# First loads, decay tables and head sums of a retention and two-layer MoE kernel

## The chip, the cores and the metric

One core of one Trainium2 chip runs the whole kernel. The metric is device time in microseconds (us), the median of several executions of the same program. Engines are named as the profile names them: PE is the matmul engine (PEld its weight loads), DVE the vector engine, ACT the scalar engine, POOL the general one, SP the engine that issues most transfers.

## The reference

Retention (attention with a decay in place of softmax) over 4 batches, 8 heads, 576 tokens and head width 64, then two dense layers over 2304 tokens of width 512. All is fp32.

```python
scores = scale * np.matmul(q, k.transpose(0, 1, 3, 2))
Dmat = np.where(rel >= 0, gamma[:, None, None] ** rel[None, :, :], 0.0)   # rel = i - j
attn = np.matmul(scores * Dmat[None], v)                 # then (tokens, 512)
h = attn @ w_in;  x = (h * np.cos(h)) @ w_out            # 512 -> 2048 -> 512
xn = x / np.sqrt(np.mean(x * x, -1) + 1e-6) * rms_g
g = xn @ w_gate                                          # 512 -> 1536
out = (g * (1.0 / (1.0 + np.exp(-g))) * (xn @ w_val)) @ w_out2
```

## The kernel before

**Retention.** Each batch is cut into five chunks of tokens, four of 128 and one of 64, so there are 20 chunks. The decay is split into factors: v is scaled once per chunk on POOL (L244) by a table in `gk_sb`, and the result is scaled on DVE (L283) by a table `gam[c]`. `gam[0]` is the loaded `gam0`; `gam[1]` to `gam[4]` are made from it on ACT, four activations each (L237), issued where the chunk is loaded. `scores(n)` makes the masked scores of a chunk: eight fp32 matmuls of contraction 64, two heads side by side on two halves of the array's rows (L249), and two DVE multiplications by the mask (L252). `values(n)` adds the chunk's sum of keys and values to `total` in PSUM (L265, four matmuls of 128x128, each covering two heads, of which only the two 64x64 blocks on the diagonal are ever read), multiplies the state of earlier chunks by q (L270), copies `total` into `state` on ACT (L275, two copies of 64x256), and adds the chunk's own part (L280, eight matmuls, one per head, with 64 weight columns each, two heads on two halves of the array's columns). An fp32 matmul appears in the profile as two matmul records.

**Order of the start.** `load(0)` brings chunk 0 in four pieces of 256 KB (keys, queries, values, keys by token), with the small tables between them, all seven on SP's queue (L226). Chunks 1 and on are one transfer of 1 MB (L228); the short chunks are two (L230, L231). Ten matmuls on a tile of ones (L290, `WARM`) run before the first data arrive. The first five chunks run in a prologue, then two chunks stand beside each of the first eight steps of the first layer.

**First layer.** A step is one tile of 512 tokens with one block of 128 of the 2048 hidden columns: products of operands split in a high and a low fp32r part, three matmuls for each (`mm3`, L187 to L189), cosine and product on DVE and ACT (L414 to L424). During the first 16 steps the weights, stored as 64-bit numbers, are turned into fp32 and split: `Block.convert`, with L132, L141 and L159 on ACT and L136, L137, L142, L143 and L124 on DVE. `split_x` (L181 and L124) splits the tokens. A scheduler lays out the order of each engine's instructions at build time by priorities and its own estimates, and each engine then works in that order; the later stages of ACT, DVE and POOL, from the end of step 15, are in an order written out by hand.

Of the kernel before, what the change touches and what calls it, by code (L numbers as in the profile page):

```python
# [22 lines left out]
F32 = mybir.dt.float32  # L23
# [3 lines left out]
AF = mybir.ActivationFunctionType  # L27
# [3 lines left out]
P = 128  # L31
B, H, S, D = 4, 8, 576, 64
# [5 lines left out]
NPAIR = H // 2  # L38
NFULL = S // P
REST = S - NFULL * P  # L40
NCH = NFULL + 1
# [18 lines left out]
NSLOT_B = NW1 - NSLOT_A  # L60
ATT_STEPS = 8
CONV_LEAD = 3
WARM = 10
AHEAD = 4
LAG = 3
LAST_BEGINS = [48, 51, 54, 65, 66, 67]
# [9 lines left out]
def body(ctx: ExitStack, tc, qkv, qkr, vr, w1, w2, rg, gq, gk, mask, out):  # L76
    nc = tc.nc
# [19 lines left out]
    psa = att.enter_context(tc.tile_pool(name="psa", bufs=1, space=PSUM, reuse_waits="tile"))  # L97
# [11 lines left out]
    def ps_tile():  # L109
        if "psh" not in late:  # L110
            return psa.tile([P, 512], F32, tag="g", bufs=3, name="g")
        taken[0] += 1
        return hidden_tile() if taken[0] % 2 else acc_tile(KC + taken[0] // 2 % 2)

    mask_sb = const.tile([P, P], F32, name="mask_sb")
# [51 lines left out]
    def temps():  # L167
        return cvp.tile([P, 2, 512], I32, tag="w", name="t")
# [32 lines left out]
    ap1 = att.enter_context(tc.tile_pool(name="ap1", bufs=1, reuse_waits="tile"))  # L201
# [3 lines left out]
    width = lambda c: P if c < NFULL else REST  # L205
    ld, sc, total = {}, {}, {}
    gam0 = ap1.tile([P, NPAIR, P], F32, name="gam0")
    gam = [gam0]
    PRO = NCH
    gk_sb = ap1.tile([P, NCH * (H + NPAIR)], F32, name="gk_sb")  # L210
    vg_sb = gk_sb[:, :NCH * H].rearrange("p (c h) -> p c h", c=NCH)
    later = gk_sb[:, NCH * H:].rearrange("p (c a) -> p c a", c=NCH)
    state = ap1.tile([P, NPAIR, P], F32, name="state")
# [5 lines left out]
    def load(n):  # L219

        b, c = chunks[n]
        x = wa.tile([P, 4, DM], F32, tag="w", name="x")
        if n == 0:
            for src, dst in ((qkv[b, c, :, 0], x[:, 0]), (qkv[b, c, :, 1], x[:, 1]), (gk, gk_sb), (mask, mask_sb),
                             (qkv[b, c, :, 2], x[:, 2]), (gq, gam0), (qkv[b, c, :, 3], x[:, 3])):
                nc.sync.dma_start(dst, src)  # L226
        elif c < NFULL:
            nc.sync.dma_start(x, qkv[b, c])  # L228
        else:
            nc.sync.dma_start(x[:, :2, :NPAIR * REST], qkr[b])  # L230
            nc.sync.dma_start(x[:REST, 2], vr[b])  # L231
        blocks = lambda a: a[:, :NPAIR * width(c)].rearrange("p (a i) -> p a i", a=NPAIR)
        ld[n] = blocks(x[:, 0]), blocks(x[:, 1]), x[:, 2], x[:, 3]
        if 0 < n < NCH:
            gam.append(ap1.tile([P, NPAIR, width(c)], F32, name=f"gam{c}"))
            for p in range(NPAIR):
                nc.scalar.activation(gam[c][:, p, :], gam0[:, p, :width(c)], AF.Copy, scale=later[:, c, p:p + 1])  # L237

    def scores(n):
        b, c = chunks[n]  # L240
# [15 lines left out]
    def values(n):  # L256
        b, c = chunks[n]
        w = width(c)
        _, qt, vv, kk = ld.pop(n)
        if c < NFULL:  # L260
            if c == 0:
                total[0] = psa.tile([P, NPAIR, P], F32, tag="st", name="total")
            for p in range(NPAIR):
                cs = slice(p * P, (p + 1) * P)
                nc.tensor.matmul(total[0][:, p, :], kk[:, cs], vv[:, cs], start=c == 0 and p == 0, stop=True,  # L265
                                 skip_group_check=True)
        po = ps_tile().rearrange("p (a i) -> p a i", a=NPAIR)
        if c > 0:
            for p in range(NPAIR):
                nc.tensor.matmul(po[:, p, :w], state[:, p, :], qt[:, p, :], start=p == 0, stop=False,  # L270
                                 skip_group_check=True)
        if c < NFULL:
            for hh in range(2):
                r = slice(hh * D, (hh + 1) * D)
                nc.scalar.copy(state[r, :, r], total[0][r, :, r])  # L275
        for p in range(NPAIR):
            for hh in range(2):
                h = 2 * p + hh
                r = slice(hh * D, (hh + 1) * D)
                nc.tensor.matmul(po[r, p, :w], vv[:w, h * D:(h + 1) * D], sc[n, hh][:w, p, :w],  # L280
                                 start=c == 0 and p == 0, stop=True, skip_group_check=True)
        t0 = b * S + c * P
        nc.vector.tensor_tensor(xall[:, :, t0:t0 + w], po[:, :, :w], gam[c], op=ALU.mult)  # L283
        del sc[n, 0], sc[n, 1]
# [3 lines left out]
    idle_bank = psp.tile([P, 512], F32, tag="acc0", name="idle_bank")  # L288
    for _ in range(WARM):
        nc.tensor.matmul(idle_bank, ones_r, warm, start=True, stop=True)  # L290
    plan = list(PLAN)

    def fetch(until):

        while plan and until not in ld:
            n = plan.pop(0)
            if n < 0:
                blocks1.append(Block(w1[len(blocks1)], wa))
            else:
                load(n)  # L300
# [3 lines left out]
    for n in range(PRO):  # L304
        fetch(n + AHEAD)
        scores(n + 1)
        values(n)
        if n == 3:
            split_x(ORDER_A[0])
            blocks1[0].convert(temps())  # L310
# [316 lines left out]
    for i in range(LAST + LAG):  # L627
# [12 lines left out]
        if i < LAST:  # L640
            t, f = steps[i]
# [278 lines left out]
```

## Time and profile before

| | us |
|---|---|
| median of 3 runs | 930.67 |
| lowest and highest run | 929.98, 932.38 |
| the profiled execution, its own time | 928.54 |
| span of that execution, first to last instruction | 926.7 |
| PE busy in the span | 903.1 |
| DVE busy in the span | 619.6 |
| ACT busy in the span | 462.2 |

The profiled execution is 2.13 us below the median and outside the range of the three runs; 1.84 us of its time lie outside the span. All stretches below are in us from the start of the span. PE is busy nearly everywhere, DVE mainly in the first 165 us, so shares over the whole span say little about the stretch in which the change lies, which is the first 130 us.

### The profile page before, as it was taken

To read this page: it belongs to the slowest core of one execution; us is meant where nothing else is said; L and a number is where in the kernel's file an instruction comes from. 1 tells how busy PE (TensorE), PEld (TensorE's weight loads), DVE (VectorE), ACT (ScalarE), POOL (GpSimd) and SP (SyncE) were. 2 spreads that over 40 slices of the span, in tenths; PEclk is the share of its full clock that TensorE was granted. 3 is DMA by queue.
4 is the path that set the end of the run, shared out by engine and by line. 5 is a ranking of instruction groups with operands and counts; after the bars stand their busy time and mean duration, and the time that the engine had idled before them with its cause. 6 is when DMAs were issued, how large, how long until landed. Compare 5 with 4: busy or idle time off the path is not lost.

```text
span 926.7 us, 12891 instructions
## 1 busy us (share of the span) xinstructions
PE 903.1 (97%) x4996; PEld 791.0 (85%) x4996; DVE 619.6 (67%) x1022; ACT 462.2 (50%) x816; POOL 26.9 (3%) x27
## 2 busy tenths in 40 slices
PE   7999999999999999999999899999999999999998
PEld 6777788888887888988888799999888999999997
DVE  3999989778888887768657666675456446333332
ACT  4656566576556666367545444444432334322222
POOL 2321100000000000000000000000000000000000
PEclk9999999999999999999999999999999999999999
DMA  8946451035424353202035376676744555755531
GB/s 334 410 186 227 155 224 72 21 117 193 164 98 159 137 159 126 69 1 103 1 148 204 124 297 251 252 268 246 259 176 176 207 209 212 265 206 209 204 132 69
DMA packets 34732, 163.72 MB, mean 177 GB/s; under 512 B 4080, under 2 KB 5232, under 8 KB 23792
## 3 DMA queue, kind: packets, MB, share of 16 engines
q1 hardware_dynamic: 34672, 162.91, 48.0%
q8 instruction: 39, 0.64, 0.3%
q14 instruction: 21, 0.17, 0.1%
HBM read 123.57 MB, written 39.32 MB: 176 GB/s over the span
## 4 chain that ended last, share of the span: by engine, by line
PE 79%; DVE 14%; ACT 4%; issue 2%; DMA 1%; SPq 0%; ACTq 0%; DVEq 0%
PE h L743 27%; PE acc L715 15%; PE acc L187 8%; PE acc L188 8%; PE acc L189 8%; PE h L189 3%; PE h L188 3%; PE h L187 3%; DVE r L421 1%; DVE t L142 1%; DVE t L143 1%; PE g L280 1%; DVE r L415 1%; PE g L249 1%; PE g L270 1%
## 5 line engine op out<-in xcount | busy, mean ns | idle before, releaser
L743 PE MATMUL h<-w 128*128 128x384 f32 x1224 | 230.5, 337 | 6.6 <-ACT s L750 2.6
L743 PEld LDWEIGHTS h<-w 128*128 128x128 f32 x1224 | 214.9, 188 | 15.2 <-ACT s L750 5.3
L715 PE MATMUL acc<-w,shi 128*128 128x512 f32 x432 | 134.3, 392 | 0.0
L187 PE MATMUL acc<-ghi,w 128*128 128x512 f32 (+1 forms) x320 | 117.4, 373 | 2.8 <-ACT xall L614 1.7
L188 PE MATMUL acc<-glo,w 128*128 128x512 f32 (+1 forms) x320 | 117.6, 369 | 0.1
L189 PE MATMUL acc<-ghi,w 128*128 128x512 f32 (+1 forms) x320 | 117.3, 368 | 0.0
L750 ACT COPY s<-h 128x384 f32<-128x384 f32 x108 | 51.9, 480 | 128.1 <-PE h L743 128.0
L715 PEld LDWEIGHTS acc<-w,shi 128*128 128x128 f32 x432 | 80.1, 188 | 13.4
L417 ACT ACTIVATE r<-r,half_pi 128x512 f32<-128x512 f32 (+1 forms) x80 | 54.5, 681 | 65.5 <-DVE r L415 65.2
L763 DVE TENSOR_TENSOR sg<-s,h 128x384 f32<-128x384 f32 x54 | 29.9, 553 | 85.6 <-PE h L743 45.4
L715 PE MATMUL acc<-w,slo 128*128 128x512 f32 x216 | 85.4, 395 | 0.0
L775 ACT CAST shi<-v 128x384 fp32r<-128x384 f32 x72 | 37.0, 514 | 70.3 <-DVE v L771 70.3
L124 DVE TENSOR_TENSOR glo<-r,ghi 128x512 fp32r<-128x512 f32 (+1 forms) x78 | 49.6, 636 | 33.4 <-ACT ghi L423 31.6
L187 PEld LDWEIGHTS acc<-ghi,w 128*128 128x128 f32 x320 | 59.4, 188 | 14.5 <-ACT xall L614 2.8
L423 ACT CAST ghi<-r 128x512 fp32r<-128x512 f32 (+1 forms) x80 | 46.2, 577 | 48.2 <-DVE r L421 46.9
L189 PEld LDWEIGHTS acc<-ghi,w 128*128 128x128 f32 x320 | 60.3, 188 | 10.1
L188 PEld LDWEIGHTS acc<-glo,w 128*128 128x128 f32 x320 | 60.3, 188 | 10.1 <-DVE glo L124 0.3
L124 DVE TENSOR_TENSOR slo<-v,shi 128x384 fp32r<-128x384 f32 x72 | 40.1, 557 | 37.3 <-ACT shi L775 37.3
L770 DVE TENSOR_TENSOR v<-s,h 128x384 f32<-128x384 f32 x54 | 29.8, 552 | 52.0 <-PE h L743 37.9
L743 PE MATMUL h<-b,w 128*128 128x384 f32 x288 | 56.8, 338 | 0.0
L188 PE MATMUL h<-xlo,w 128*128 128x512 f32 (+1 forms) x148 | 54.3, 367 | 0.1
L189 PE MATMUL h<-xhi,w 128*128 128x512 f32 (+1 forms) x148 | 54.2, 366 | 0.0
(105 smaller groups left out, 1518.6 us busy)
## 6 DMA issues: line engine op xcount, KB each, us to landing
w<-s SPq DMA_DIRECT2D x24, 1024.0 KB, 4.8
raw<-w_dram SPq DMA_DIRECT2D x36, 512.0 KB, 4.0
w<-w SPq DMA_DIRECT2D x18, 1024.0 KB, 5.1
w<-s SPq DMA_DIRECT2D x24, 768.0 KB, 6.4
raw<-w_dram SPq DMA_DIRECT2D x16, 1024.0 KB, 7.1
x<-qkv_dram SPq DMA_DIRECT2D x15, 1024.0 KB, 8.1
s<-w SPq DMA_DIRECT2D x12, 1024.0 KB, 4.8
s<-w SPq DMA_DIRECT2D x12, 768.0 KB, 3.6
```

The source lines that it names most:

```text
L124: eng.tensor_tensor(dst, src, hi.bitcast(F32), op=ALU.subtract)
L187: nc.tensor.matmul(dst, a[0], b[0], start=start, stop=False)
L188: nc.tensor.matmul(dst, a[0], b[1], start=False, stop=False)
L189: nc.tensor.matmul(dst, a[1], b[0], start=False, stop=stop)
L417: nc.scalar.activation(r, r, AF.Sin, bias=half_pi, scale=1.0)
L423: nc.scalar.copy(hi, r)
L715: nc.tensor.matmul(acc, (hi, hi, lo)[k][:, c], w[:, u, (0, 1, 0)[k], :], start=start and u == 0 and k == 0, stop=stop and u == 1 and k == 2)
L743: nc.tensor.matmul(bank, a[:, wp], xp[:, c], start=start and kc == 0 and n == 0, stop=kc == 1 and n == 2, skip_group_check=True)
L750: nc.scalar.copy(t, alpha)
L763: nc.vector.tensor_tensor(t, s, bank, op=ALU.add)
L770: nc.vector.tensor_tensor(t, s, bank, op=ALU.add)
L775: nc.scalar.copy(hi, t)
```

## The change

The first chunk comes in two transfers of 512 KB on SP's queue, and the three tables go out on ACT's queue, beside them. Chunk 1 comes in two halves, each with a semaphore of its own. The warm-up has eight matmuls in place of ten. The decay tables are written out after `values(n)` in place of at the load. The head sums are eight matmuls of 64x64 in place of four of 128x128: `total` is half as wide, each head writes its own half of the partitions, and ACT reads a contiguous block. Work on DVE and POOL keeps its count and its sizes.

```diff
-WARM = 10
+WARM = 8
...
         if n == 0:
-            for src, dst in ((qkv[b, c, :, 0], x[:, 0]), (qkv[b, c, :, 1], x[:, 1]), (gk, gk_sb), (mask, mask_sb),
-                             (qkv[b, c, :, 2], x[:, 2]), (gq, gam0), (qkv[b, c, :, 3], x[:, 3])):
-                nc.sync.dma_start(dst, src)
+            for eng, src, dst in ((nc.sync, qkv[b, c, :, :2], x[:, :2]), (nc.scalar, gk, gk_sb),
+                                  (nc.scalar, mask, mask_sb), (nc.sync, qkv[b, c, :, 2:], x[:, 2:]),
+                                  (nc.scalar, gq, gam0)):
+                eng.dma_start(dst, src)
+        elif n == 1:
+            nc.sync.dma_start(x[:, :2], qkv[b, c, :, :2])
+            nc.sync.dma_start(x[:, 2:], qkv[b, c, :, 2:])
...
-        if 0 < n < NCH:
-            gam.append(ap1.tile([P, NPAIR, width(c)], F32, name=f"gam{c}"))
-            for p in range(NPAIR):
-                nc.scalar.activation(gam[c][:, p, :], gam0[:, p, :width(c)], AF.Copy, scale=later[:, c, p:p + 1])
+
+    def decay(c):
+
+        gam.append(ap1.tile([P, NPAIR, width(c)], F32, name=f"gam{c}"))
+        for p in range(NPAIR):
+            nc.scalar.activation(gam[c][:, p, :], gam0[:, p, :width(c)], AF.Copy, scale=later[:, c, p:p + 1])
+
+    half = lambda hh: slice(hh * D, (hh + 1) * D)
...
-                total[0] = psa.tile([P, NPAIR, P], F32, tag="st", name="total")
+                total[0] = psa.tile([P, NPAIR, D], F32, tag="st", name="total")
             for p in range(NPAIR):
-                cs = slice(p * P, (p + 1) * P)
-                nc.tensor.matmul(total[0][:, p, :], kk[:, cs], vv[:, cs], start=c == 0 and p == 0, stop=True,
-                                 skip_group_check=True)
+                for hh in range(2):
+                    h = 2 * p + hh
+                    cs = slice(h * D, (h + 1) * D)
+                    nc.tensor.matmul(total[0][half(hh), p, :], kk[:, cs], vv[:, cs], start=c == 0 and p == 0,
+                                     stop=True, skip_group_check=True)
...
         values(n)
+        if n + 1 < NCH:
+            decay(n + 1)
```

The scheduler's order moves with it. First SP and ACT at the start of the program; `x` is a chunk of q, k and v, `raw` a block of weights, `gam_91` the loaded table. Before, SP's first rows are:

```order
L226 DMA x<-qkv_dram 128x512 x2
L226 DMA gk_sb<-gk_dram 128x60
L226 DMA mask_sb<-mask_dram 128x128
L226 DMA x<-qkv_dram 128x512
L226 DMA gam_91<-gq_dram 128x512
L226 DMA x<-qkv_dram 128x512
L228 DMA x<-qkv_dram 128x2048 x3
L151 DMA raw<-w_dram 128x2048
```

Now SP's are:

```order
L227 DMA x<-qkv_dram 128x1024 x2
L229 DMA x<-qkv_dram 128x1024
L230 DMA x<-qkv_dram 128x1024
L232 DMA x<-qkv_dram 128x2048 x2
L151 DMA raw<-w_dram 128x2048
```

Chunk 1 stands third and fourth on SP's queue, where it stood eighth. ACT's first rows before, with the decay tables at L237 and the copies of `total` at L275:

```order
L237 ACT_TABLE_LOAD
L237 ACTIVATE gam_121<-gam_91,gk_sb 128x128 x4
L237 ACTIVATE gam_143<-gam_91,gk_sb 128x128 x4
L237 ACTIVATE gam_150<-gam_91,gk_sb 128x128 x4
L237 ACTIVATE gam_160<-gam_91,gk_sb 128x64 x4
L275 COPY state<-total 64x4x64 x4
L132 ACTIVATE t<-raw 128x1024
```

ACT's first rows now, where the tables are L243 and the copies L284:

```order
L227 DMA gk_sb<-gk_dram 128x60
L227 DMA mask_sb<-mask_dram 128x128
L227 DMA gam_91<-gq_dram 128x512
L243 ACT_TABLE_LOAD
L243 ACTIVATE gam_178<-gam_91,gk_sb 128x128 x4
L243 ACTIVATE gam_224<-gam_91,gk_sb 128x128 x4
L243 ACTIVATE gam_272<-gam_91,gk_sb 128x128 x4
L243 ACTIVATE gam_318<-gam_91,gk_sb 128x64 x3
L284 COPY state<-total 64x4x64 x2
L243 ACTIVATE gam_318<-gam_91,gk_sb 128x64
L284 COPY state<-total 64x4x64 x2
```

Three transfers are issued ahead of the table load, and one of the sixteen activations has moved behind the first copies; fifteen still stand ahead of them. PE in the first two chunks, before:

```order
L290 MATMUL idle_bank<-warm,ones_r 128x512 x10
L249 MATMUL g<-x 128x128 x8
L265 MATMUL total<-x 128x128 x4
L249 MATMUL g<-x 128x128 x8
L280 MATMUL g<-s_137,x 64x128
...
L265 MATMUL total<-x 128x128 x2
```

PE there now, where the lines are L298, L257, L275 and L288:

```order
L298 MATMUL idle_bank<-warm,ones_r 128x512 x8
L257 MATMUL g<-x 128x128 x16
L275 MATMUL total<-x 64x64 x8
L288 MATMUL g<-s_129,x 64x128
...
L275 MATMUL total<-x 64x64 x8
L257 MATMUL g<-x 128x128 x8
```

The scores of chunk 1 have moved ahead of the head sums of chunk 0. From there to the last chunk the rows of PE, DVE and ACT keep their kinds and counts, but many stand a few places earlier or later; behind the first 16 steps of the first layer the three engines' orders are the same as before.

## Rows read from the trace of the kernel before

**Rows 1.** Busy time in four stretches: length, each engine's busy us, clock, DMA.

```profile
0.00:20.00 20.00, 14.24 (x130) 11.63 (x130) 6.14 (x12) 8.05 (x22) 4.57 (x9) 1.00 0.88 323
20.00:120.00 100.00, 95.66 (x862) 79.26 (x859) 96.67 (x124) 59.74 (x84) 19.33 (x16) 0.98 0.63 239
120.00:165.00 45.00, 44.64 (x231) 37.03 (x230) 41.10 (x54) 29.65 (x38) 0.00 (x0) 1.00 0.39 153
165.00:926.70 761.70, 748.54 (x3782) 663.10 (x3780) 475.71 (x834) 364.72 (x673) 2.99 (x2) 1.00 0.46 166
```

**Rows 2.** Chain of work that ended last: start, length, what ran.

```profile
3.07 4.95 DMA gam<-gq_dram
...
35.24 0.43 PE g L189
...
119.51 0.57 issue
120.08 0.69 DVE xall L283
```

**Rows 3.** Timeline of the first 22 us: start, length, instruction, idle before.

```profile
2.10 4.59 PE L290 MATMUL idle_bank<-warm,ones_r 128*128 128x512 f32 x10 [2.10 <-DVE warm L287]
...
4.02 1.54 SPq L228 DMA_DIRECT2D x<-qkv_dram  x3
...
8.10 1.28 ACT L237 ACT_TABLE_LOAD   x1 [8.10 <-DMA gam<-gq_dram]
...
9.39 4.57 ACT L237 ACTIVATE gam<-gam,gk_sb 128x128 f32<-128x128 f32 x16
...
11.48 1.16 PE L249 MATMUL g<-x 64*128 64x128 f32 x16 [1.32 <-DMA x<-qkv_dram]
...
14.75 0.68 PE L265 MATMUL total<-x 128*128 128x128 f32 x4 [1.09 <-ACT state L275]
...
19.16 1.15 ACT L132 ACTIVATE t<-raw 128x1024 f32<-128x1024 f32 x1 [0.25 <-DMA raw<-w_dram]
...
21.41 0.90 DVE L136 TENSOR_SCALAR t<-t 128x1024 f32<-128x1024 f32 x1
```

**Rows 4.** Single microseconds of the start; last two columns DMA share and GB/s.

```profile
2.00:3.00 1.00, 0.90 (x2) 0.83 (x3) 0.00 (x0) 0.00 (x0) 0.00 (x0) 1.00 0.75 260
3.00:4.00 1.00, 1.00 (x4) 0.71 (x3) 0.00 (x0) 0.00 (x0) 0.00 (x0) 1.00 0.90 279
4.00:5.00 1.00, 1.00 (x4) 0.81 (x3) 0.00 (x0) 0.00 (x0) 0.00 (x0) 1.00 0.79 215
5.00:6.00 1.00, 1.00 (x3) 0.79 (x3) 0.00 (x0) 0.00 (x0) 0.00 (x0) 1.00 0.87 203
6.00:7.00 1.00, 1.00 (x8) 0.38 (x8) 0.00 (x0) 0.00 (x0) 0.00 (x0) 1.00 0.86 236
...
9.00:10.00 1.00, 0.97 (x8) 0.97 (x8) 0.10 (x1) 0.99 (x4) 0.00 (x0) 1.00 1.03 434
```

**Rows 5.** Timeline of PE: groups of one shape in a dense stretch.

```profile
20.11 1.16 PE L265 MATMUL total<-x 128*128 128x128 f32 x8
...
21.10 1.06 PE L270 MATMUL g<-x,state 128*128 128x128 f32 x8
...
22.09 1.09 PE L280 MATMUL g<-s,x 128*64 128x128 f32 x16
...
23.11 0.68 PE L249 MATMUL g<-x 64*64 64x64 f32 x16
...
23.73 1.16 PE L265 MATMUL total<-x 128*128 128x128 f32 x8
```

**Rows 6.** Longest waits of PE between 20 and 120 us: total, times, longest.

```profile
PE g L249 <- DVE r L421: 1.3, 1, 1.3
PE g L280 <- DVE s L252: 1.2, 1, 1.2
```

**Rows 7.** PE around a slow stretch: length, PE busy, granted clock, DMA.

```profile
35.00:36.00 1.00, 1.00 (x4) 0.50 1.05 444
```

More of the change, by code (lines that the diff above doesn't have):

```diff
@@ L273, in values @@
             for hh in range(2):
-                r = slice(hh * D, (hh + 1) * D)
-                nc.scalar.copy(state[r, :, r], total[0][r, :, r])
+                nc.scalar.copy(state[half(hh), :, half(hh)], total[0][half(hh)])
         for p in range(NPAIR):
@@ L278, in values @@
                 h = 2 * p + hh
-                r = slice(hh * D, (hh + 1) * D)
-                nc.tensor.matmul(po[r, p, :w], vv[:w, h * D:(h + 1) * D], sc[n, hh][:w, p, :w],
+                nc.tensor.matmul(po[half(hh), p, :w], vv[:w, h * D:(h + 1) * D], sc[n, hh][:w, p, :w],
                                  start=c == 0 and p == 0, stop=True, skip_group_check=True)
```

## The prediction

> **What bounds the kernel now.** I read the busy times by stretch first, then the chain of work that ended last, then the timeline of the start, then the waits. After 120 us PE is the bound: busy 44.64 of 45 us and then 748.54 of 761.7 [rows 1], and no instruction behind the first 16 steps changes its place. So the change can only decide how early that stretch begins, and a gain there is carried to the end. The hand-over is in the chain: at 120.08 us a DVE multiplication (L283) runs that PE waits for, and from there the chain is PE's [rows 2]. Between 20 and 120 us neither engine is alone the bound: DVE is busy 96.67 of 100 us and PE 95.66 [rows 1]. DVE has 3.33 us of idle time there, PE 4.34. They wait for each other in turn; PE's two longest waits there are both for DVE, 1.3 and 1.2 us [rows 6]. Before 20 us the bound is the arrival of data and of the decay tables. PE waits 1.32 us for chunk 1 at 11.48 us; the sums of chunk 1 wait until 14.75 us for ACT to copy the sums of chunk 0, and ACT is late because it began the tables only at 8.10 us, when `gam0` had landed, and worked on them until 13.96 (9.39 + 4.57) [rows 3]; the transfer of `gam0`, 4.95 us, heads the chain [rows 2]. The first conversion starts on ACT at 19.16 us, 0.25 us late for its block of weights, and on DVE at 21.41 us [rows 3].
>
> **Start, the transfers.** The bytes are the same, so what can be gained is the time in which the transfer engines were empty or slow. From 2 to 7 us the five rows move 260 + 279 + 215 + 203 + 236 GB/s times 1 us, that is 1.19 MB, at shares of 0.75 + 0.90 + 0.79 + 0.87 + 0.86, so 4.17 us of 5 are filled; from 9 us on the rate is 434 GB/s [rows 4]. Two bounds follow. If the new pieces only fill the empty part, everything behind them comes 0.83 us earlier. If pieces of 4 KB a row run at the rate of the 8 KB rows, 434 x 5 us is 2.17 MB, 0.98 MB more, which is worth 0.98 / 0.434 = 2.3 us. No row of before shows a piece of 4 KB a row; I take 1.8, nearer the upper end, because SP's queue no longer holds chunk 1 back. Before, it was issued at 4.02 us [rows 3] behind seven others; now it stands behind two, each about 0.46 us (4.02 less a start at 0.8, over seven), so at some 1.7 us.
>
> The Trainium skill bears on this. Its page "DMA: Bandwidth & Descriptors", section "Issuing engines are not separate DMA queues", says that transfers of all issuing engines run on the same 16 engines and that several issuers only save issue time. By that rule alone the term would be the empty 0.83 us and not 1.8, and the sum 1.0 us smaller. The trace speaks neither for nor against it, since before all transfers here were SP's; that rates differ with the row length is another matter, which the rule leaves open.
>
> **Start, the tables.** `gam0` is now ACT's third transfer in place of SP's sixth. Its issue moves from 3.07 us [rows 2] to about 1.7 us (two issues of 0.46 us ahead of it), so with the same 4.95 us to landing ACT starts 1.4 us earlier; if it lands in some 3 us, 3.3 earlier. Fifteen activations in place of sixteen stand ahead of the first copy, 4.57 / 16 = 0.29 us each [rows 3]. So the copy comes 1.7 to 3.6 us earlier, and the sums of chunk 1, which waited 1.09 us for it, with it. That writing `decay` behind `values` does not move the tables behind the copies costs nothing as long as the transfers are the later of the two. Both paths have to move for the conversions to start earlier, so the smaller one counts: **1.8 us**, between 0.8 and 2.3.
>
> **The warm-up.** Ten matmuls take 4.59 us [rows 3], so two less are 0.9 us. The first scores may start so much earlier, but the next thing PE can do is wait for chunk 1, now ahead of the sums of chunk 0. I count it at nothing; the wait for chunk 1 covers it. Were that cover gone, it would add up to 0.9 us to the gain.
>
> **Head sums.** Four matmuls of 128x128 take 0.99 us from their start to that of the next group (20.11 to 21.10) [rows 5]. The new eight have 64 weight columns and 64 streamed columns, and no row shows this shape with 128 rows of contraction. Two rows bound it. Eight matmuls with 128 rows and 64 weight columns, which stream 128, take 1.02 us (22.09 to 23.11); eight with 64 of everything take 0.62 (23.11 to 23.73) [rows 5]. A streamed length of 64 decides, I think, since two heads lie on two halves of the columns in both, so I take 0.62. That saves 0.37 us a chunk, between a loss of 0.03 and 0.37. Sixteen chunks have sums (four in each of four batches), two before 20 us, so fourteen are left, 14 x 0.37 = 5.2 us of PE's time between 20 and 120 us.
>
> The page "TensorE: Matmul & The Clock Gate" of the Trainium skill, section "LDWEIGHTS (loading the stationary operand)", puts a weight load at its columns over 1.2, in ns. Sixteen loads of 64 columns, one after another, would be 16 x 53 = 0.85 us by an estimate from that page, which leaves a saving of 0.14 us a chunk; the sum below would then be about 0.9 us smaller. The row of the small scores speaks against it: sixteen loads of 64 columns and their matmuls are done in 0.62 us, so two halves load side by side.
>
> Little of the 5.2 us reaches the end. Where PE waits for DVE the time goes into a longer wait. It counts only where DVE waits for PE or for what hangs on PE, and DVE has only 3.33 us of idle time to give. DVE's share of the two engines' idle time is 3.33 / (3.33 + 4.34) = 0.43; I take that share of the 3.33, **1.4 us**. The ends are 3.3 us, and, since the scheduler has moved many rows of DVE and ACT by a few places, a loss of one more wait like PE's longest, 1.3 us [rows 6]. What is late next is DVE, which converts weights without a gap worth naming.
>
> The copies of the sums on ACT read the same 64x256 elements and stay at nothing; POOL and the later transfers keep their count, and the later weights' transfers follow the slots that PE frees, so they move along.
>
> **Sum.** 1.8 + 1.4 = 3.2 us. From the profiled execution that is 928.54 - 3.2 = 925.3. That execution is 2.13 us under the median of the runs, so against the median the forecast is 930.67 - 3.2, **927.5 us**. Between the ends of the terms, 0.8 - 1.3 = -0.5 and 2.3 + 3.3 = 5.6, lie 931.2 and 925.1.
>
> **Rivals.** (1) *DVE keeps the time.* The start moves by its lower end, and the saving on PE is lost or eaten by a new wait between PE and DVE. For it: DVE is busy 96.67 of 100 us [rows 1], and PE's two longest waits are for DVE [rows 6]. Against it: nothing on DVE has grown, and its start hangs on the data. 0.8 us of gain with nothing from the sums is 929.9; with half a wait lost, some 930.5. (2) *More than forecast, by the clock.* From 35 to 36 us the granted clock is 0.50, the 1.2 GHz level [rows 7], and the matmuls take 0.43 us each [rows 2]; the chain runs through them. The mean over 20 to 120 us is 0.98 [rows 1], so some 2 us of PE's time are lost there. If PE is busier ahead of that stretch in the new order and the clock does not fall, up to 2 us come back, and the time is 925.5. Against it: PE has less work in the stretch, so it can also pause more. (3) *Slower: the clock stays low at the start.* The ten warm matmuls ran at 0.46 us each, the pace of the low level, although the clock column reads 1.00 there [rows 3, 4]; the scores behind them ran at the full pace. Now the warm-up is two shorter, and PE then waits for chunk 1. If the clock is not raised before that wait, PE's work up to 20 us, 14.24 - 4.59 = 9.65 us [rows 1, 3], takes twice as long; PE's idle time there behind the first 2.10 us, 20 - 14.24 - 2.10 = 3.66 us, takes up a part, and 6.0 us remain. Less the gain of 3.2 that is 2.8 us slower, 933.5. It outweighs the gain once 3.66 + 3.2 = 6.9 us of PE's work run at the low level, that is if it lasts to some 17 us. Against it: the scores follow the warm-up without a break, so PE is busy from 2.1 to nearly 7 us as before. (4) *The order of the tables does nothing*: it is part of the forecast already, since ACT's rows show it.
>
> **How the numbers follow.** A measurement of this kernel tells about 0.3%, 2.8 us, from no change. The forecast (926 to 929) has a chance of 0.50, rival 1 (929 to 931.5) 0.24, rival 2 (924 to 926) 0.16, rival 3 (932 and more) 0.10. The border of a gain of 0.3% is 927.9, close to the middle of the forecast, so 0.34 of its 0.50 and all of rival 2 are faster, 0.50; 0.40 is no change that can be told, 0.10 slower. The range takes in the forecast, nearly all of rival 1 and most of rival 2: 924.3 to 931.2.
>
> **What would show it.** The sums as eight matmuls in about 0.62 us a chunk; chunk 1's scores at 8 to 10 us in place of 11.48; the sums of chunk 1 near 12 us in place of 14.75; ACT's first conversion near 17.4 us in place of 19.16 and DVE's near 19.6; DVE busy more than 97% of the 100 us behind that, PE less than before; the hand-over to PE 3 us before 120. Wrong would be: a start that is earlier and a hand-over at 120 us (rival 1); no stretch at 0.50 near 35 us (rival 2); scores of chunk 1 that take more than 2 us (rival 3); sums that take 1 us.

## The result

The changed kernel takes 934.61 us (median of 9 runs, 932.86 to 939.33) beside 930.71 us for the kernel before (9 runs, 927.1 to 932.38). The ratio is 1.0053, with an interval of 1.0032 to 1.0074. It is slower by some 4.9 us by the ratio (3.9 us between the medians), where the forecast was 3.2 us faster, and outside the range. The execution that was profiled took 939.33 us, the slowest of its nine, and the profiled one of before was a quick one, so the two traces stand further apart (10.5 us of span) than the medians, and what a difference between them is worth is read from medians only.

Busy time in the four stretches of [rows 1], of the changed kernel (length, then busy us of PE, PEld, DVE, ACT and POOL with their counts, granted clock, DMA share, GB/s):

```profile
0.00:20.00 20.00, 12.50 (x109) 10.44 (x110) 5.33 (x11) 6.58 (x19) 4.71 (x10) 0.86 0.91 342
20.00:120.00 100.00, 90.41 (x887) 73.04 (x887) 88.50 (x113) 53.53 (x75) 20.42 (x15) 0.91 0.63 233
120.00:165.00 45.00, 44.77 (x304) 36.89 (x305) 40.90 (x53) 31.15 (x41) 1.04 (x1) 1.00 0.41 158
165.00:937.20 772.20, 758.99 (x3828) 671.60 (x3826) 486.86 (x848) 370.67 (x681) 3.00 (x2) 1.00 0.46 164
```

The last stretch is 10.5 us longer only because the same work starts later. Between 20 and 120 us DVE was busy 8.2 us less than before, and PE 5.3 us less: both stood idle more, and the clock was lower (0.91, before 0.98). The chain of work that ended last runs through ACT and DVE here, to the last xall but two (start, length, what):

```profile
120.86 1.16 ACT t L132
122.02 0.94 ACT w L159
122.98 1.73 DVE w L124
...
130.61 0.61 DVE xall L291
131.27 1.16 PE g L280 x8
```

The hand-over of [rows 2], 120.08 us, is now at 130.61 us.

**The start.** Timeline of the changed kernel (start, length, instruction, idle before and what ended it), beside [rows 3]:

```profile
8.92 1.16 PE L257 MATMUL g<-x 64*128 64x128 f32 x16 [1.21 <-DMA x<-qkv_dram]
9.40 1.28 ACT L243 ACT_TABLE_LOAD   x1 [9.40 <-DMA gam<-gq_dram]
...
10.70 4.33 ACT L243 ACTIVATE gam<-gam,gk_sb 128x128 f32<-128x128 f32 x15
...
14.93 0.74 ACT L284 COPY state<-total 64x256 f32<-64x256 f32 x2
...
15.77 1.12 PE L275 MATMUL total<-x 128*64 128x64 f32 x16 [4.20 <-issue]
...
24.36 0.69 DVE L136 TENSOR_SCALAR t<-t 128x1024 f32<-128x1024 f32 x1
```

The scores of chunk 1 stand at 8.92 us in place of 11.48, as forecast. But ACT's tables begin 1.30 us later than before, the copy ends later, and the sums of chunk 1 run at 15.77 us in place of 14.75, behind a pause of 4.20 us. The first conversion on DVE is at 24.36 us in place of 21.41. The cause is in the list of transfers (destination, source, issuing queue, KB, us from issue to landing):

```profile
gam<-gq_dram ACTq DMA_DIRECT2D x1, 256.0 KB, 7.7
mask_sb<-mask_dram ACTq DMA_DIRECT2D x1, 64.0 KB, 5.4
```

`gam0` was issued at 1.66 us, 1.4 us earlier, and took 7.7 us in place of 4.95 [rows 2].

**The transfers.** Single microseconds, beside [rows 4]:

```profile
4.00:5.00 1.00, 1.00 (x4) 0.81 (x3) 0.00 (x0) 0.00 (x0) 0.00 (x0) 1.00 1.01 383
5.00:6.00 1.00, 1.00 (x5) 0.35 (x5) 0.00 (x0) 0.00 (x0) 0.00 (x0) 1.00 1.03 404
6.00:7.00 1.00, 1.00 (x10) 1.00 (x12) 0.00 (x0) 0.00 (x0) 0.51 (x1) 1.00 1.01 392
```

With 267 and 222 GB/s in the two microseconds ahead of these, 1.67 MB moved from 2 to 7 us in place of 1.19.

**The sums.** PE's timeline in a dense stretch, beside [rows 5]:

```profile
23.05 0.69 PE L275 MATMUL total<-x 128*64 128x64 f32 x16
23.67 1.16 PE L280 MATMUL g<-x,state 128*128 128x128 f32 x8
```

From the start of the sums to the next group it is 0.62 us, before 0.99.

**The waits.** PE's longest wait between 20 and 120 us was 1.3 us [rows 6]. Now the view has, for that stretch (total, times, longest):

```profile
PE g L280 <- DVE s L260: 5.2, 3, 3.7
```

The timeline around the longest of the three:

```profile
57.84 1.22 DVE L142 SCALAR_TENSOR_TENSOR t<-raw,t 128x1024 int32<-128x1024 int32 x1
...
59.58 1.22 DVE L143 CUSTOM_DVE_ANT_0 t<-raw,t 128x2048 uint16<-128x2048 uint16 x1
...
60.72 1.28 DVE L260 TENSOR_TENSOR s<-g,mask_sb 128x512 f32<-128x512 f32 x2
...
61.45 1.57 PE L280 MATMUL g<-x,state 128*128 128x128 f32 x8 [3.68 <-DVE s L260]
```

Chunks are counted from 0, except where the text says third or ninth. The masked scores `s` of chunk 8 read their scores out of PSUM, and the state products of chunk 7 come next in that ring of buffers, so they wait until `s` is made. On DVE the two multiplications stand behind all but the last step of a weight conversion (L136, L137, L142, L143). DVE's rows in the order of before have them between those steps (`s0` stands one row ahead of these):

```order
L124 TENSOR_TENSOR w_525<-t_518,w_525 128x2x512
L137 TENSOR_SCALAR t_528<-t_528 128x1024
L252 TENSOR_TENSOR s1_578<-g_567,mask_sb_78 128x512
L142 SCALAR_TENSOR_TENSOR t_528<-raw_412,t_528 128x1024
L415 SCALAR_TENSOR_TENSOR r_559<-r_559,g_546 128x512
L143 ISA t_528<-raw_412,t_528 128x2048
L421 TENSOR_TENSOR r_559<-g_546,r_559 128x512
L283 TENSOR_TENSOR xall_84<-g_587,gam2_143 128x4x128
L124 TENSOR_TENSOR w_535<-t_528,w_535 128x2x512
```

DVE's rows in the changed kernel, with both behind L143:

```order
L137 TENSOR_SCALAR t_549<-t_549 128x1024
L142 SCALAR_TENSOR_TENSOR t_549<-raw_425,t_549 128x1024
L425 SCALAR_TENSOR_TENSOR r_580<-r_580,g_567 128x512
L143 ISA t_549<-raw_425,t_549 128x2048
L260 TENSOR_TENSOR s0_597<-g_587,mask_sb_78 128x512
L260 TENSOR_TENSOR s1_599<-g_588,mask_sb_78 128x512
L124 TENSOR_TENSOR w_556<-t_549,w_556 128x2x512
L431 TENSOR_TENSOR r_580<-g_567,r_580 128x512
L291 TENSOR_TENSOR xall_84<-g_612,gam2_224 128x4x128
```

**The clock.** It was granted at the level of 0.50 (1.2 GHz) from 14.26 to 21.08, 34.74 to 41.56, 62.04 to 65.46 and 79.11 to 85.94 us, 23.9 us in all; before, from 33.85 to 37.26 [rows 7]. Each list is of the one execution that was profiled: the mean granted clock of the changed kernel's nine executions is 0.987 to 0.994, and 0.987 in this one; that of the 128 executions of the kernel before that ran beside the experiments is 0.992 to 1.0, and 0.998 in the profiled one. Two of the single microseconds:

```profile
16.00:17.00 1.00, 1.00 (x18) 0.88 (x18) 0.00 (x0) 0.04 (x1) 0.22 (x1) 0.50 1.09 414
...
64.00:65.00 1.00, 1.00 (x11) 0.67 (x8) 0.03 (x1) 1.00 (x2) 0.00 (x0) 0.50 0.90 377
```

### The profile page after: what moved, and what is told of

The parts are those of the page before. It is cut to its first block, busy times and chain, and to the rows that moved or that the text cites. A ratio compares the mean times of both kernels' runs of the same rounds, so it can differ in the third digit from the quotient of the medians.

```text
span 937.2 us, 13136 instructions
## 1 busy us (share of the span) xinstructions
PE 906.7 (97%) x5122; PEld 792.0 (85%) x5122; DVE 621.6 (66%) x1022; ACT 461.9 (49%) x816; POOL 29.2 (3%) x27
## 4 chain that ended last, share of the span: by engine, by line
PE 71%; DVE 20%; ACT 5%; issue 2%; DMA 1%; SPq 0%; POOL 0%; ACTq 0%; DVEq 0%
PE h L753 26%; PE acc L725 15%; PE acc L187 6%; PE acc L188 6%; PE acc L189 6%; PE h L188 2%; PE h L189 2%; PE h L187 2%; DVE t L142 2%; DVE r L425 2%; DVE r L431 2%; DVE t L143 2%; DVE glo L124 2%; ACT ghi L433 2%; PE g L288 1%
```

## The experiments

There were three theories, A and B from the outset and C from E5 on: **A**, the late `gam0` on ACT's queue delays the tables and all behind them; **B**, the new order that the scheduler lays out puts what PE waits for behind weight conversions; **C**, PE has less to do with the shorter sums, pauses more, and its clock falls. Ratios are against the kernel before, run beside them on the same chip.

**Parts alone, each in the order that its own build gives.**

E1: `gam0` on SP's queue, between the halves of chunk 0.

```diff
-                                  (nc.scalar, mask, mask_sb), (nc.sync, qkv[b, c, :, 2:], x[:, 2:]),
-                                  (nc.scalar, gq, gam0)):
+                                  (nc.scalar, mask, mask_sb), (nc.sync, gq, gam0),
+                                  (nc.sync, qkv[b, c, :, 2:], x[:, 2:])):
```

> One edit to the changed kernel: the table gam0 goes out on SP's queue between the two halves of chunk 0, in place of ACT's queue. The order of PE and DVE stays that of the changed kernel. Theory A (the loss begins with the tables: on ACT's queue gam0 landed 7.7 us after its issue, the copy of the first sums came at 14.93 us, PE paused 4.2 us and its clock fell to 0.5 from 14.26 to 21.08 us): gam0 lands near 5.5 us, the copy comes near 11.5 us, the scores of chunk 2 take 1.2 us in place of 2.08, the first conversion on DVE starts 4 to 5 us earlier than 24.36, and the median falls from 934.6 by 3 to 5 us, to 930 or 931. Theory B (the loss lies in the new order of DVE and PE behind 45 us): the start is earlier, but the median stays within 1.5 us of 934.6.

931.99 us, ratio 1.0025 (1.001 to 1.004). PE, DVE and ACT keep the order of the changed kernel. `gam0` landed after 5.1 us, the table load began at 6.35 us and the sums of chunk 1 at 12.72. That is between what A (930 to 931) and B (above 933) had: A is worth 2.6 us of the medians, and half of the loss stays.

E2: the changed kernel with four 128x128 sums again. E3: the kernel before with the eight 64x64 sums alone.

```diff
-                for hh in range(2):
-                    h = 2 * p + hh
-                    cs = slice(h * D, (h + 1) * D)
-                    nc.tensor.matmul(total[0][half(hh), p, :], kk[:, cs], vv[:, cs], start=c == 0 and p == 0,
-                                     stop=True, skip_group_check=True)
+                cs = slice(p * P, (p + 1) * P)
+                nc.tensor.matmul(total[0][:, p, :], kk[:, cs], vv[:, cs], start=c == 0 and p == 0, stop=True,
+                                 skip_group_check=True)
```

> The changed kernel with the head sums as before, four matmuls of 128x128; transfers, warm-up and tables as changed. Theory A (late tables and the clock behind the pause): the pause of PE near 12 to 16 us and the low clock stay, the median is 933 to 936, like the changed kernel. Theory B (the sums' shorter matmuls change the scheduler's order, DVE puts conversions ahead of masked scores, PE waits 3.7 us near 58 us): that wait goes and the median is 929 to 931.

> The kernel before with the head sums alone as eight matmuls of 64x64; transfers, tables and warm-up as before. Theory A: the start is that of before, nothing pauses longer, so the median is 929 to 931. Theory B: the wait of PE near 58 us is there and the median is 933 to 936. Both: eight matmuls in 0.6 us a chunk.

E2 took 937.93 us, 1.0084 (1.0062 to 1.0107); E3 934.16 us, 1.0044 (1.0025 to 1.0064). Either half alone loses too. E2 lies above what A and B gave for it; its trace has both a pause of 3.5 us ahead of the sums of chunk 1 and waits of PE for `s` of 5.0 us in all, and why it is slower than the whole was not followed up. E3 starts as the kernel before does, so A cannot be its cause; it has the same wait:

```profile
PE g L274 <- DVE s L254: 4.7, 2, 3.6
```

E4: ten warm-up matmuls again (`WARM = 10`).

> The changed kernel with ten warm matmuls in place of eight. If the shorter warm-up matters by the level of the clock in the first 20 us, the clock is at 1.0 there and the median falls by 2 us or more; theory A says that the fall of the clock comes from the pause of 4.2 us in front of the sums of chunk 1, which this edit leaves, so the median stays within 1.5 us of 934.6.

934.38 us, 1.0044 (1.0023 to 1.0065): no difference that can be told from the changed kernel. The warm-up counts nothing, as forecast.

**The order alone.** A table of ranks for each engine holds PE, DVE and ACT, over the first 16 steps, in a chosen order; the work is untouched. Four kernels: the changed one in the order of before (E5), E1 in it (E6), E3 in it (E7), and the kernel before in the order of the changed one (E8). The edit, in all four:

```diff
+ORDER = {"PE": [8, 9, 10, 11, 12, 13, 14, 15, 24, 25,
...
+        for first, then in zip(ranks, ranks[1:]):
+            tc.add_manual_dep(made[then], made[first].name,
```

> The changed kernel as it is, but PE, DVE and ACT are held, up to the end of the first 16 steps, in the order that the scheduler gave the kernel before (edges of order alone between instructions; the eight sums stand where the four stood). gam0 still goes out on ACT's queue. Theory B (the new order makes PE wait 3.7 us for masked scores near 58 us, and the clock falls behind that): that wait goes, the median falls by about 2 us, to 932 or 933; what is left over the kernel before is the start with its late tables. Theory C (shorter sums leave PE emptier, so the clock falls whatever the order): the median stays within 1 us of 934.4, the clock has three or more stretches at 0.5.

> As the run before, and gam0 on SP's queue between the halves of chunk 0 besides. Theories A and B together (late tables cost 2.5 us, the order costs the rest): nothing is left of the loss and the start is about 2 us earlier, so the median is 926 to 929, 1.5 to 4 us under the kernel before. Theory C: 931 to 933, like the run with gam0 on SP's queue alone (931.99).

> The kernel before with the eight shorter sums alone, held in the order of the kernel before. Theory B: the loss of the sums alone (934.16 against 930.3) was all order, so the median is 929 to 930.5. Theory C: it stays at 933 to 935.

> The kernel before, with its own transfers, tables, warm-up and sums, held in the order that the scheduler gave the changed kernel. Theory B: the wait of PE for masked scores near 55 us appears, with a stretch at 0.5 behind it, and the median is 932.5 to 935. Theory C: the order is harmless with the longer sums, the median is within 1 us of 930.3.

| kernel | us | ratio | interval |
|---|---|---|---|
| E5 changed, order of before | 929.86 | 0.9998 | 0.9986 to 1.001 |
| E6 as E1, order of before | 929.37 | 0.9988 | 0.9978 to 0.9997 |
| E7 sums only, order of before | 930.09 | 1.0003 | 0.9986 to 1.002 |
| E8 before, order of the changed one | 933.99 | 1.0036 | 1.0022 to 1.0051 |

B holds: every edit in the old order loses nothing that can be told, and the untouched program in the new order loses 3.4 us by the ratio (3.2 between the medians). In E8's trace the wait is there without any of the edits:

```profile
PE g L319 <- DVE s L301: 4.1, 1, 4.1
```

(E8 also pauses 4.4 us at the start for chunk 1, whose scores the new order puts ahead of the first sums while the loads are the old ones; E15 below prices a late start.) The late `gam0` costs nothing that can be told once the order is the old one (E5 beside E6). And the expected gain is missing there too: E6, the quickest, gains 0.12% (0.03 to 0.22).

**Where in the order?** E9 takes the changed kernel in its own order, and E10 takes E1, with one pair of moves: chunk 8's last four score matmuls directly behind its first four on PE, and its two masked-score multiplications back between the steps of the conversion. Rows of DVE, as the order has them before and behind the move:

```diff
 TENSOR_SCALAR t<-t 128x1024
+TENSOR_TENSOR s_597<-g,mask_sb 128x512
 TENSOR_SCALAR t<-t 128x1024
+TENSOR_TENSOR s_599<-g,mask_sb 128x512
 SCALAR_TENSOR_TENSOR t<-raw,t 128x1024
 SCALAR_TENSOR_TENSOR r<-r,g 128x512
 ISA t<-raw,t 128x2048
-TENSOR_TENSOR s_597<-g,mask_sb 128x512
-TENSOR_TENSOR s_599<-g,mask_sb 128x512
```

> The changed kernel, held in its own order of the engines' instructions, except for chunk 8: its last four score matmuls stand directly behind its first four, and its two masked-score multiplications stand directly behind the two conversions that they stood behind in the kernel before. If that one moved pair is what the new order costs, TensorE's wait of 3.68 us at 61.45 us is gone, the low clock behind it too, and the time is 934.6 less 2 to 3.7, so 931 to 932.5 us. If the cost is spread over the whole new order, the wait shrinks and the time stays at 933.5 to 934.6 us.

> The same two moves in the kernel that also loads gam0 on SyncE's queue (931.99 us with the wait of 4.55 us in it). If the wait and the late load are the whole loss, 928.5 to 930.5 us, near the 929.4 us of the same edits in the order of before. If the order costs in other places too, 931 to 932 us.

934.83 us, 1.0038 (1.0023 to 1.0053), and 932.93 us, 1.0024 (1.0008 to 1.0041): nothing gained. E9 also shows that holding an order by a table does not itself bring E5 to E7 their time. The timeline of E9 shows why:

```profile
62.49 0.75 ACT L335 COPY state<-total 64x256 f32<-64x256 f32 x2
...
63.38 0.45 PE L326 MATMUL total<-x 128*64 128x64 f32 x2 [3.10 <-ACT state L335]
```

The wait of 3.68 us for `s` is short now, and PE waits 3.10 us a little later, for the copies of chunk 7's state, which stand on ACT behind an activation and a weight cast in the new order.

E13 and E14 split the order by engines, on E1: only PE's as before, and only DVE's and ACT's as before.

> The changed kernel with gam0 on SyncE's queue (931.99 us in its own order, 929.37 us in the order of the kernel before on TensorE, VectorE and ScalarE), here with TensorE's instructions in the order of before and VectorE's and ScalarE's in their own new order. If the new order costs where TensorE's matmuls stand (scores of later chunks split and put behind others), the time is 929 to 930 us; if it costs on VectorE (masked scores and xall put behind the conversions of the weights), it stays at 931.5 to 932.5 us.

> The other half of the same: TensorE in the new order, VectorE and ScalarE in the order of before. If VectorE's order is what costs, 929 to 930 us; if TensorE's is, 931.5 to 932.5 us; if the cost comes from the two together, both halves lie between, at 930 to 931.5 us, or a half is even slower than the whole, because the two orders no longer fit each other.

933.04 us, 1.0016 (1.0002 to 1.003), and 950.19 us, 1.0197 (1.0177 to 1.0218). With PE's old order and the others' new one, PE still waits 5.19 us at 58.23 us for `s`. The other half is worse than the whole: taken apart, the three orders no longer fit each other, so an engine's order could not be priced by itself here.

E16 and E17 add a second move to E9 and E10: chunk 7's state copies directly behind the first activation of r. E18 adds a third to E17: the subtraction that makes the low part of a weight goes behind the r and the xall on DVE.

```diff
 ACTIVATE r<-g,quarter 128x512
+COPY state<-total 64x4x64 x2
 ACTIVATE r<-r,half_pi 128x512
 CAST w<-t 128x2x512
-COPY state<-total 64x4x64 x2
...
-TENSOR_TENSOR w<-t,w 128x2x512
 TENSOR_TENSOR r<-g,r 128x512
 TENSOR_TENSOR xall<-g,gam_224 128x4x128
+TENSOR_TENSOR w<-t,w 128x2x512
```

> The changed kernel in its own order with chunk 8's score matmuls and masked scores moved as before (934.83 us), and also chunk 7's two state copies on ScalarE moved from behind the second activation of r and a weight cast to directly behind the first activation of r, where they stood in the kernel before. In the trace without this move TensorE waited 3.1 us at 63.38 us for them. If that chain of two waits is the order's cost, the time falls by 2 to 3.5 us, to 931.3 to 932.8 us; if the next thing in line takes the wait over (the masked scores of the later chunks, the weight conversions on VectorE), less than 1 us is gained and it stays at 934 to 934.8 us.

> The same three moves with gam0 on SyncE's queue (932.93 us without the move of the state copies, 929.37 us in the order of the kernel before). If the two waits are the order's cost, 929.4 to 930.5 us; if the cost is passed on to the next wait, 932 to 933 us.

> The kernel with gam0 on SyncE's queue and chunk 8's scores and chunk 7's copies moved (932.77 us), and on VectorE one more move: the subtraction that makes the low part of a weight (which waits 1.1 us for ScalarE's cast) stands behind the r and the xall that it stood ahead of, as in the kernel before. In the trace without it TensorE waits 3.95 us at 61.23 us for that r. The r can then run some 2.2 us earlier. If this third link is the last of the chain, the time falls by 1.5 to 2.5 us, to 930.2 to 931.3 us; if the wait moves on a fourth time, it stays at 932.3 to 933.3 us, and the cost belongs to the new order as a whole.

E16 took 935.45 us, 1.0051 (1.0037 to 1.0064), and E17 932.77 us, 1.0023 (1.0014 to 1.0033): again nothing. In E17 the wait has gone over to a third place:

```profile
59.35 1.22 DVE L175 TENSOR_TENSOR w<-t,w 128x1024 fp32r<-128x1024 f32 x1 [1.11 <-ACT w L210]
60.49 0.68 DVE L482 TENSOR_TENSOR r<-g,r 128x512 f32<-128x512 f32 x1
...
61.23 1.11 PE L308 MATMUL g<-x 64*64 64x64 f32 x8 [3.95 <-DVE r L482]
```

DVE itself waits 1.11 us for ACT's cast while the r behind it, which holds a bank that PE needs, could run. With the third move, in E18:

```profile
58.84 0.68 DVE L482 TENSOR_TENSOR r<-g,r 128x512 f32<-128x512 f32 x1
...
59.57 1.11 PE L308 MATMUL g<-x 64*64 64x64 f32 x8 [1.62 <-DVE r L482]
...
60.04 1.21 DVE L175 TENSOR_TENSOR w<-t,w 128x1024 fp32r<-128x1024 f32 x1
```

E18 took 930.42 us, ratio 0.9993 (0.998 to 1.0006). The wait did not move on, and the loss is gone, 2.35 us below E17 by the medians with one DVE instruction moved by two places. So with `gam0` on SP's queue the cost of the new order lies in the waits between 54 and 64 us that the three moves shorten. That all three are needed is read from the traces, in which one wait stood behind another: the third move without the first two was not tried, nor were the three in the changed kernel itself.

**Where did the gain go?** E11 is E6 with the old long sums; E12 is E6 with eight matmuls of ones in each of four pauses of PE before 32 us; E15 is the kernel before, in its own order, with 30 warm-up matmuls in place of 10.

```diff
-WARM = 10
+WARM = 30
...
+            nc.tensor.matmul(idle_bank[:, :P], ones_r, ones_r, start=True, stop=True)
```

> The new first loads with gam0 on SyncE's queue, four old 128x128 head sums for each chunk, everything held in the order of the kernel before. It differs from the 929.37 us kernel in the sums alone. If the shorter sums empty TensorE and its clock falls for it (the theory for the gain that is missing), the granted clock is low for no longer than before (3.4 us) and the time is 928.0 to 929.3 us, at or below the one with the short sums. If the short sums bring their matmul time as forecast, this one is slower by 1 to 3 us: 930.4 to 932.4 us.

> The 929.37 us kernel (new loads, gam0 on SyncE's queue, short sums, old order) with eight matmuls of 128 columns of ones, whose result nobody reads, put into four of TensorE's pauses: before the sums of chunk 1 (pause 1.07 us), before the sums of chunk 3 (1.23 us), before the state products of chunk 3 (1.44 us) and behind the sums of chunk 5 (1.12 us). If the falls of the clock follow from these pauses, the stretches at half clock from 25.0 to 28.4 and from 35.2 to 38.7 us are gone, and the time falls by 1 to 3 us, to 926.4 to 928.4 us. If they do not, or if the time at half clock is hidden by other waits, the time stays at 929 to 930 us.

> The kernel before, held in its own order, with 30 warm-up matmuls in place of 10: the first scores start some 4.6 us later, at about 11.2 us, and the first xall stands some 2 us later than 13.9 us. If the loads set the pace of the first 45 us (the chunk's v-scaling on GpSimd starts at the same time in every kernel), the lead is made up by about chunk 4 and the time is that of before within 0.5 us. If the start is on the path, as the forecast had it, the 2 us stay: 932 to 933 us.

E11 took 931.14 us, 0.9995 (0.9981 to 1.001). The median lies on the side on which the short sums bring their time, but the interval overlaps that of E6, so the sums make no difference that can be told; C had E11 at or below E6, and its median is above.

E12 took 930.18 us, 0.9988 (0.9973 to 1.0004), as E6. Yet the clock followed the pauses, as C says. Busy time, clock and transfers in E6 from 20 to 40 us:

```profile
20.00:30.00 10.00, 7.33 (x91) 6.36 (x89) 6.41 (x8) 3.86 (x8) 4.48 (x3) 0.83 1.01 420
30.00:40.00 10.00, 8.66 (x66) 6.71 (x65) 9.52 (x12) 6.14 (x10) 2.09 (x2) 0.83 1.02 385
```

The same stretches in E12:

```profile
20.00:30.00 10.00, 9.21 (x128) 8.10 (x128) 7.66 (x10) 5.48 (x9) 4.27 (x3) 1.00 1.02 419
30.00:40.00 10.00, 8.83 (x89) 7.10 (x86) 9.93 (x14) 6.92 (x11) 2.26 (x2) 1.00 1.02 396
```

With the pauses filled the clock stays up until 58.5 us, and the time does not fall. So the two falls ahead of 40 us that E12 removes cost nothing that can be told. And C does not explain the loss, since E8 has it with the long sums.

For the missing gain C stays open in part, because one fall is left in E12, from 58.5 to 65.3 us. E6 has it from 59.1 to 66.0 us, from inside a pause of PE on:

```profile
60.19 1.11 PE L308 MATMUL g<-x 64*64 64x64 f32 x8 [2.18 <-DVE r L482]
...
61.23 2.07 PE L331 MATMUL g<-x,state 128*128 128x128 f32 x8
...
63.24 1.98 PE L339 MATMUL g<-s,x 128*64 128x128 f32 x16
...
65.26 0.69 DVE L342 TENSOR_TENSOR xall<-g,gam 128x512 f32<-128x512 f32 x1 [2.07 <-PE g L339]
```

The last two groups of matmuls took 1.16 and 1.09 us in the trace of before; the clock was up there, and DVE waited for no matmul between 54 and 80 us. In E6 DVE waits 2.07 us for them, and so it does, 2.1 us, in the traces of E11, E12 and E15. The executions point the same way. Of the 128 executions of the kernel before, the 35 with a mean granted clock of 0.994 have a median of 931.69 us, the 48 with 0.996 one of 930.67, the 29 with 0.998 one of 929.94, the eight with 1.0 one of 928.38. Whether the low clock makes them longer, or the pauses that it follows do, no run separates. E5, E6 and E7 have a median clock of 0.994 and the kernel before 0.996, which goes with about 1 us. No run holds the clock up near 60 us, so how much of the missing gain went there is not shown.

E15 took 930.0 us, 0.9992 (0.9978 to 1.0006). The first sums stood at 12.98 us in place of 9.03, the first xall at 16.47 in place of 13.88:

```profile
12.98 1.16 PE L289 MATMUL total<-x 128*128 128x128 f32 x8
...
16.47 0.68 DVE L307 TENSOR_TENSOR xall<-g,gam 128x512 f32<-128x512 f32 x1
```

A start on PE that is 4 us later costs nothing that can be told. The longer warm-up has changed the clock too: the median of the mean clocks is 0.998 in E15 and 0.996 in the kernel before, which by the executions above goes with about 1 us, so a cost of that size may be hidden. The v-scaling on POOL shows when a chunk has landed. POOL's timeline of the kernel before, at its third chunk and its ninth:

```profile
13.95 1.04 POOL L244 TENSOR_TENSOR x<-x,gk_sb 128x512 f32<-128x512 f32 x1 [1.40 <-DMA x<-qkv_dram]
...
35.62 1.05 POOL L244 TENSOR_TENSOR x<-x,gk_sb 128x512 f32<-128x512 f32 x1 [3.66 <-DMA x<-qkv_dram]
```

The changed kernel, the same two:

```profile
12.74 1.04 POOL L252 TENSOR_TENSOR x<-x,gk_sb 128x512 f32<-128x512 f32 x1 [1.46 <-DMA x<-qkv_dram]
...
35.28 1.24 POOL L252 TENSOR_TENSOR x<-x,gk_sb 128x512 f32<-128x512 f32 x1 [3.41 <-DMA x<-qkv_dram]
```

E6, the ninth:

```profile
36.10 1.04 POOL L303 TENSOR_TENSOR x<-x,gk_sb 128x512 f32<-128x512 f32 x1 [3.86 <-DMA x<-qkv_dram]
```

E15, the ninth:

```profile
36.66 1.04 POOL L268 TENSOR_TENSOR x<-x,gk_sb 128x512 f32<-128x512 f32 x1 [3.87 <-DMA x<-qkv_dram]
```

The changed kernel's lead of 1.21 us at the third chunk is 0.34 at the ninth; E6, with the start as it was meant, is 0.48 behind there. The transfer engines' share is 1.00 to 1.03 in the stretches from 10 to 20 and from 20 to 35 us in the kernel before, in the changed one and in E6, so the stream of loads has no room in which a lead could grow. And E15's ninth chunk is 1.04 us late without a cost that can be told, so within a microsecond the loads do not seem to be the bound either. Behind them it is DVE, by its busy time: from 80 to 100 and from 100 to 120 us it is busy 19.85 and 19.96 us of 20 in the kernel before, and in E6:

```profile
80.00:100.00 20.00, 19.29 (x206) 15.40 (x206) 19.97 (x27) 14.39 (x20) 3.29 (x2) 1.00 0.57 200
100.00:120.00 20.00, 19.49 (x198) 15.55 (x196) 19.94 (x26) 11.36 (x16) 3.59 (x3) 1.00 0.46 174
```

Matmul time that is saved on PE there can only lengthen its waits for DVE. Between 60 and 80 us DVE is not full in E6 (15.90 us, before 18.95); its longest wait there is the one for PE at the low clock, above. What in detail takes the lead away ahead of the ninth chunk was not followed up.

## Why the prediction was wrong

**The step that failed is the price of the new order.** The prediction saw that many rows of DVE and ACT had moved, and bounded it by "one more wait like PE's longest, 1.3 us [rows 6]", as the low end of the term. Measured, the new order costs 3.4 us in the untouched program (E8). The bound was taken from a trace in which the order kept that very wait short: the rows named in [rows 6], PE waiting for DVE's `r` and `s`, are the waits that grew to 3.95 and 3.68 us. And it was taken for one wait, where three lay behind one another in the traces of the changed kernel, E9 and E17.

**The tables: sign wrong.** Taking the issue time to be 1.4 us earlier was right (1.66 us). The transfer from issue to landing was put at 3 to 4.95 us and took 7.7, so the path of the tables, forecast 1.7 to 3.6 us earlier, came 1.0 us later. The rule that the later of the two paths counts was right; it counted against the change. With `gam0` on SP's queue the sums of chunk 1 do come 2.0 us earlier than before (E1), as the lower part of the forecast had it. In the new order that placement is worth 2.6 us of the medians, in the old one nothing that can be told.

**The transfers: right, but worth nothing.** The rise from 1.19 to 1.67 MB is 0.48 / 0.434 = 1.1 us, within 0.83 and 2.3 and below the 1.8 taken; chunk 1's v-scaling comes 1.27 us earlier (10.23 for 11.50). That this would be carried to the end was wrong: E6 shows that an earlier start brings at most 0.22%, and by E15 one 4 us later costs at most some 1.6 us, an estimate (0.06% at the end of its interval, and about 1 us for its higher clock). The prediction had read DVE's idle time and the waits, but not asked whether the load stream, at a share of 1.0 for 30 us behind the start, would let a lead live.

The Trainium skill says in "DMA: Bandwidth & Descriptors", section "Issuing engines are not separate DMA queues", that transfers issued by any engine run on the same 16 engines, and that a second issuer saves issue time alone. The trace agrees: `gam0` was issued 1.4 us earlier on ACT's queue and took longer to land than on SP's (7.7 and 5.1 us in E1). By this rule the prediction would have had 0.83 us for the term of the transfers; the trace gives 1.1.

**The sums: size right, value wrong.** 0.62 us was forecast for a chunk's sums and 0.62 measured. The row that it was taken from has its two heads on two halves of the array's rows (L249), not of the columns as the prediction says, so that it held for halves of the columns was in part luck. Of the 5.2 us of PE's time 1.4 were counted; E7 gives 1.0003, at most 0.14% of gain, and E11 beside E6 no difference. DVE's share of idle time was no measure of what it could give. What became of the rest is open in part: the low clock near 60 us, above, may hold some of it.

**The warm-up**: counted at nothing, and E4 agrees. It did show at one place: chunk 0's scores took 1.93 us in the changed kernel and 1.16 before and in E4.

**The rivals.** (1), DVE keeps the time, 929.9 to 930.5 us, fits by its number what the edits do in the old order (929.4 to 930.1). (2) falls for the stretch near 35 us: with the clock up until 58.5 us nothing is gained (E12). (3) named a time near the measured one, 933.5, by another cause, so its nearness is luck: chunk 1's scores ran at the full pace (1.16 us at 8.92 us), and the warm-up has no part in the loss (E4). The slower side had 0.10; a rival "the new order makes PE wait behind conversions" was missing, although the difference of DVE's orders held the rows that told it.

## What to carry to other kernels

Where a scheduler lays out the order, an edit is two changes: the work, and the new order. Hold the old order and time the edit in it, and hold the new order and time the old program in it; here the edit was worth at most 0.22% and the order 3.4 us. A wait that is small in the trace is small because of the order of that trace, so it is no bound for another order; look in the difference for rows that free a buffer and now stand behind work that is itself waiting. And before an earlier start is counted, delay the start: if that costs little, an earlier one will bring little. Look at the granted clock of such a pair of runs, too; the edit that delays can also change it.

## What was not expected of the hardware

A transfer of 256 KB on ACT's queue, issued beside two of 512 KB on SP's, took 7.7 us to land; on SP's own queue, between the two, 5.1 us (E1) and 5.0 (E6). The 64 KB table beside it took 5.4 us in place of 3.1 before.

PE's clock fell to the lower level inside or after pauses of PE. In the changed kernel it was low from 14.26 us, while PE paused for 4.20 us, to 21.08. In E12, where matmuls that nobody reads filled the pauses, it was up until 58.5 us at the same time of the kernel, so the falls of E6 ahead of 40 us cost nothing that can be told. That every fall is free is not shown: in the one near 60 us DVE waits 2.07 us for PE in E6, and the executions of the kernel before are the longer the lower their mean clock (medians of 928.38 us at 1.0 and 931.69 at 0.994).
